# Residual and second-layer sums added by accumulating GpSimd DMAs, in a fused state-space and Mish feed-forward kernel

## The chip, the cores and the metric

The kernel runs on one core of one Trainium2 chip. The metric is the device time of one execution in microseconds; the time before is 371.92 us, the median of three runs (371.62 to 372.28). The engines are TensorE (PE in the profile, with PEld for its weight loads), VectorE (DVE), ScalarE (ACT), GpSimd (POOL) and SyncE (SP), which only issues DMAs.

## The reference

A sequence x of 2048 rows and 640 channels is normalized over the channels; two branches of the normalized rows are added to x: an S4D state-space convolution and a dense layer, Mish, dense layer.

```python
def _A_ref(u, log_A_real, A_imag, C_real, C_imag, log_dt, D_skip):
    ...
    P = jnp.exp((A * dt[:, None])[:, :, None] * pos[None, None, :])
    K = 2.0 * jnp.einsum("dn,dnl->dl", C, P).real
    ...
    return y + u * D_skip[None, None, :]      # y: causal convolution of u with K
...
def _B_ref(x, w1, b1, w2):
    h = jnp.einsum("bsd,df->bsf", x, w1) + b1
    sp = jnp.log1p(jnp.exp(-jnp.abs(h))) + jnp.where(h > 0, h, jnp.zeros_like(h))
    act = h * jnp.tanh(sp)
    return jnp.einsum("bsf,fd->bsd", act, w2)
...
x = A_u
xn = _layernorm(x, axis=-1)
return x + _A_ref(xn, ...) + _B_ref(xn, ...)
```

The layers are 640 to 1728 and 1728 to 640. With the given parameters the convolution's kernel is so smooth that a branch of the program replaces it by running sums: two prefix sums per channel with two coefficients. A flag computed from the parameters decides at the end whether a general branch has to run; here it does not.

## The kernel before

**Tiling.** All work is held transposed: channels or hidden units on the 128 partitions, rows of the sequence along the free dimension. The sequence is cut into four blocks b of 512 rows (TB), the 640 channels into five tiles k of 128 (KD), the 1728 hidden units into 14 chunks f (NF; one of them has 64). A step (b, f) is one hidden chunk of one block. Every float32 operand of a matmul is split into a high and a low float16 part, and three products (high-high, low-high, high-low) are summed, so that a step has 15 matmuls of 512 columns for the first layer (mm1) and 15 for the second (mm2).

**Order within a step.** The program order on each engine is written out by hand in step(b, f): the loads of that step (lists LOADS, all on SP), mm1(b, f), mm2 of the chunk three steps earlier (LAG = 3), the Mish operations of chunk f and the rest of those of chunk f - 1, and the lists V_, A_ and W_, in which place() puts side work for DVE and ACT. Engines are in-order queues. In the first three steps of a block mm2 still finishes the last three chunks of the block before; in step 2 the last of them, so that the five accumulators ACC[k] (one PSUM bank each) are then complete sums of the block before. The mm2 of the new block's first chunk overwrites them in step 3, after mm1(b, 3).

**Joining.** In step 2 of a block, join(b - 1, k) empties ACC[k]. For most tiles it adds ACC[k] / SO to RES[b, k], a buffer of 128x512 float32 into which SP loaded the residual x in good time (load_res). For the tiles in the set EARLY it is drain: it adds ACC[k] / SO to the tile XT[b][:, k], which by then holds everything else, and SP stores the result to the output.

**The skip work (state-space branch and residual).** XT[b][:, k] holds the normalized, transposed rows. For each of the 20 tiles, at the steps listed in CONV, four functions run:

- skip_a, a step before on ACT: two scaled copies g1 and g0 of XT, and the carry from the block before;
- skip_b on DVE: the first prefix sum, in g1, and XT = XT * D + RES, where RES holds x, or x and the second layer's sum if the join came first;
- skip_c on DVE: the second prefix sum, in g0, and XT = XT + g0; if the tile isn't EARLY, SP stores XT to the output;
- skip_d, a step later on ACT: the new carries.

CONV puts the tiles of block 0 at steps (1, 4) to (1, 7) and (2, 0), those of block 1 at (2, 3) to (2, 7), those of block 2 at (2, 13) and (3, 3) to (3, 6), those of block 3 at (3, 7) to (3, 11). EARLY are the tiles whose skip work lies in their own block: (2, 0) and all of block 3.

**The next block's rows.** In steps 2 to 5 of a block DVE takes mean and variance of the next block's rows (stats). In step 5 rstds() runs three small operations on GpSimd (lines 404, 405 and 743): 1/sigma by a power, and a copy of the means. In step 7, behind mm1, PE transposes that row of statistics (spread, line 411), ACT copies it out, and SP writes it to DRAM and reads it back broadcast to all partitions (bc). From step 8 on DVE normalizes one tile of XT a step with it (norm_t), and the float16 parts of the next block follow (hi_x, lo_x). In the middle of the program GpSimd does nothing else.

**The end.** Behind the last step PE finishes the last chunks tile by tile; drain empties each of the five tiles of block 3 when its accumulator is complete, the last one in two halves, and SP stores them.

Of the kernel before, what the change touches and what calls it, by code (L numbers as in the profile page):

```python
# [13 lines left out]
F32 = mybir.dt.float32  # L14
F16 = mybir.dt.float16
I32 = mybir.dt.int32
AF = mybir.ActivationFunctionType
OP = mybir.AluOpType
AX = mybir.AxisListType

P = 128
# [4 lines left out]
TB = 512  # L26
NB = L // TB
NT = TB // P
KD = D // P
# [3 lines left out]
LAST = NF - 1  # L33
HALF = 8
LAG = 3
# [12 lines left out]
SH, SO = SX * S1, SA * S2  # L48
# [238 lines left out]
def body(ctx: ExitStack, tc: tile.TileContext, x, xT, logA, Aim, Cr, Ci, logdt, vec, w1, w1T, w2, w2T, out):  # L287
    nc = tc.nc
    v, a, pe, sp, g = nc.vector, nc.scalar, nc.tensor, nc.sync, nc.gpsimd
# [11 lines left out]
    row = pool("row", 2)  # L301
# [19 lines left out]
    cc = cst.tile([P, 6, KD], F32, name="cc")  # L321
# [23 lines left out]
    ACC = [ps.tile([P, TB], F32, name=f"acc{k}") for k in range(KD)]  # L345
    W1S, W2S, XT, RES, XROW, ACT, SM, NX, CHK, SK, ML = ({} for _ in range(11))
    NCHK = NF + 3 * KD

    def load_w1(f, queues=(sp,)):
        W1S[f] = row.tile([P, KD, P], F32, name="w1s", tag="w", bufs=8)  # L350
        n, m = FC[f], P // len(queues)
        for j, e in enumerate(queues):
            o = D * FO[f] + j * m * KD * n
            e.dma_start(W1S[f][j * m:(j + 1) * m, :, :n], w1[o:o + m * KD * n].rearrange("(p k f) -> p k f", p=m, k=KD))

    def load_w2(f):
        W2S[f] = row.tile([P, D], F32, name="w2s", tag="w", bufs=8)
        n = FC[f]
        sp.dma_start(W2S[f][:n], w2[FO[f]:FO[f] + n])
        if n < P:  # L360
            sp.dma_start(W2S[f][n:2 * n], w2[FO[f]:FO[f] + n])

    def load_x(b, i):
        XROW[b, i] = row.tile([P, D], F32, name="xrow", tag="x", bufs=4)
        sp.dma_start(XROW[b, i], xr[b, i])

    def load_res(b, k):
        RES[b, k] = row.tile([P, TB], F32, name="res", tag="r", bufs=7)
        sp.dma_start(RES[b, k], xT[k * P:(k + 1) * P, b * TB:(b + 1) * TB])


    def hi_w1(f):
        n = FC[f]
        a.activation(W1H[f][:, :, :n], W1S[f][:, :, :n], AF.Copy, scale=S1)

    def lo_w1(f, e=v):
        n = FC[f]
        e.scalar_tensor_tensor(W1L[f], W1S.pop(f)[:, :, :n], S1, W1H[f][:, :, :n], op0=OP.mult, op1=OP.subtract)

    def hi_w2(f):  # L380
        a.activation(W2H[f], W2S[f], AF.Copy, scale=S2)

    def lo_w2(f, e=v):
        e.scalar_tensor_tensor(W2L[f], W2S.pop(f), S2, W2H[f], op0=OP.mult, op1=OP.subtract)

    def hi_x(b, k):
        a.activation(XH[b % 2][k], XT[b][:, k], AF.Copy, scale=SX)
# [5 lines left out]
    def xt_alloc(b):  # L393
        XT[b] = big.tile([P, KD, TB], F32, name="xt", tag="big" + "ACBA"[b])
# [30 lines left out]
    def load_par():  # L425
        t = big.tile([P, 4, KD, NS], F32, name="par", tag="bigB")
        for j, src in enumerate((logA, Aim, Cr, Ci)):
            sp.dma_start(t[:, j], src.rearrange("(k p) n -> p k n", p=P))
        return t
# [76 lines left out]

    def skip_b(b, k):
        g1, _ = SK[b, k]
        xt = XT[b][:, k]
        v.tensor_tensor_scan(g1[:, 1:], g1[:, 1:], zero.to_broadcast([P, TB]), car[:, 1, k:k + 1], op0=OP.add, op1=OP.add)  # L510
        v.scalar_tensor_tensor(xt, xt, cc[:, 3 * (b == 0) + 2, k:k + 1], RES.pop((b, k)), op0=OP.mult, op1=OP.add)  # L511

    def skip_c(b, k):
        g1, g0 = SK[b, k]
        v.tensor_tensor_scan(g0, g0, g1[:, 0:TB], car[:, 0, k:k + 1], op0=OP.add, op1=OP.add)  # L515
        v.tensor_tensor(XT[b][:, k], XT[b][:, k], g0, op=OP.add)
        if (b, k) not in EARLY:
            sp.dma_start(out[k * P:(k + 1) * P, b * TB:(b + 1) * TB], XT[b][:, k])

    def skip_d(b, k):  # L520
        g1, g0 = SK.pop((b, k))
        a.copy(car[:, 1, k:k + 1], g1[:, TB:])
        a.copy(car[:, 0, k:k + 1], g0[:, TB - 1:])
# [123 lines left out]
    def drain(b, k, src, t=slice(0, TB)):  # L647
        z = XT[b][:, k, t]
        v.scalar_tensor_tensor(z, src[:, t], 1 / SO, z, op0=OP.mult, op1=OP.add)
        sp.dma_start(out[k * P:(k + 1) * P, b * TB + t.start:b * TB + t.stop], z)  # L650

    def join(b, k):
        if (b, k) in EARLY:
            drain(b, k, ACC[k])
        else:
            v.scalar_tensor_tensor(RES[b, k], ACC[k], 1 / SO, RES[b, k], op0=OP.mult, op1=OP.add)

    E_, A_, V_, W_ = ({(b, f): [] for b in range(NB) for f in range(NF)} for _ in range(4))  # L660
    LOADS = {(b, f): [] for b in range(NB) for f in range(NF)}
    PEX = {}

    def place():
        for f in range(NF):

            if f + 6 < NF:
                LOADS[0, f].append(lambda f=f: load_w1(f + 6))
            if f + 2 < NF:
                LOADS[0, f].append(lambda f=f: load_w2(f + 2))  # L670
            A_[0, f].append(lambda f=f: hi_w2(f))
            if f + 4 < NF:
                A_[0, f].append(lambda f=f: hi_w1(f + 4))
            if f > 0 and f + 3 < NF:
                V_[0, f].append(lambda f=f: lo_w1(f + 3))
            V_[(0, f + 1) if f < LAST - 1 else (1, f - LAST + 1)].append(lambda f=f: lo_w2(f))

        LOADS[0, 4].append(lambda: SM.update(ops=mode_ops(load_par())))
        for at, n in (((0, 6), 13), ((0, 7), 15), ((1, 0), 8), ((1, 1), 99)):
            W_[at].append(lambda n=n: [o() for _, o in zip(range(n), SM["ops"])])  # L680

        LOADS[1, 0].append(lambda: xt_alloc(0))
        for k, f in enumerate((0, 0, 1, 1, 3)):
            V_[1, f].append(lambda k=k: v.tensor_tensor(XT[0][:, k], XH[0][k], XL[0][k], op=OP.add))

        for b in range(NB - 1):
            for i in range(NT):
                LOADS[b, i].append(lambda b=b, i=i: load_x(b + 1, i))
                W_[b, i + 2].append(lambda b=b, i=i: stats(b + 1, i))
            LOADS[b, 5].append(lambda b=b: load_xt(b + 1))  # L690
            W_[b, 5].append(rstds)
            PEX[b, 7] = spread
            for k in range(KD):
                W_[b, 8 + k].append(lambda b=b, k=k: norm_t(b + 1, k, NX["bc"]))
                (E_ if k == KD - 1 else A_)[b, 9 + k].insert(0, lambda b=b, k=k: hi_x(b + 1, k))
                (V_ if k == KD - 1 else W_)[b, 9 + k].insert(0, lambda b=b, k=k: lo_x(b + 1, k))

        n = [(b, f) for b in range(1, NB) for f in range(NF)][2:]
        for j in range(NCHK):
            LOADS[n[max(j - 3, 0)]].append(lambda j=j: load_chk(j))  # L700
            A_[n[j]].append(lambda j=j: chk(j))
        W_[n[NCHK]].append(lambda: [o() for o in chk_end()])
        PEX[n[NCHK + 2]] = ok_sum
        W_[n[NCHK + 2]].append(ok_end)

        for b in range(1, NB):
            for k in range(KD):
                (V_ if k < 3 else W_)[b, LAG - 1].append(lambda b=b, k=k: join(b - 1, k))

        for at, c, k in CONV:  # L710
            b, f = at
            prev = (b, f - 1) if f else (b - 1, LAST)
            nxt = (b, f + 1) if f < LAST else (b + 1, 0)
            if c == b:
                LOADS[b, f - 2].append(lambda c=c, k=k: load_res(c, k))
            A_[prev].append(lambda c=c, k=k: skip_a(c, k))
            V_[at].append(lambda c=c, k=k: skip_b(c, k))
            W_[at].append(lambda c=c, k=k: skip_c(c, k))
            A_[nxt].insert(0, lambda c=c, k=k: skip_d(c, k))
        for b in range(NB - 1):  # L720
            for k in range(KD):
                if (b, k) not in EARLY:
                    LOADS[b, LAST].append(lambda b=b, k=k: load_res(b, k))

    CONV = [((1, 4 + k), 0, k) for k in range(4)] + [((2, 0), 0, 4)] + [((2, 3 + k), 1, k) for k in range(KD)]
    CONV += [((2, 13), 2, 0)] + [((3, 2 + k), 2, k) for k in range(1, KD)] + [((3, 7 + k), 3, k) for k in range(KD)]
    EARLY = {(c, k) for (b, _), c, k in CONV if c == b}

    def stats(b, i):
        if i == 0:  # L730
            NX["mv"] = tmp.tile([P, NT, 2], F32, name="mv")
            NX["st"] = tmp.tile([P, 2, NT], F32, name="st_row")
        for o in stat_ops(NX["mv"], XROW.pop((b, i)), i):
            o()
# [183 lines left out]
    b, k = NB - 1, KD - 1  # L918
# [47 lines left out]
```

## Time and profile before

| what | value |
|---|---|
| time, median of three runs | 371.92 us (371.62 to 372.28) |
| the profiled execution's own time | 371.5 us |
| its span, first to last instruction | 369.6 us |
| granted TensorE clock, mean | 0.996 |
| DMA moved | 40.81 MB, mean 110 GB/s |
| DMA queue of SP (q1): share of the 16 engines' time | 33.8% |

A row of a group names the line, the engine, the operation, the tile written and the tiles read with partitions x elements, the count, the busy time in us, the mean ns of one, and the idle time of the engine just before them with what ended most of it. A row of waits names who waited for whom: us in total, times, the longest. A row of a stage gives its length, busy time and count of PE, PEld, DVE, ACT and POOL, the granted clock, the share of DMA and GB/s. A row of a timeline gives start and length in us; what stands in brackets is the idle time before it and what ended it. A matmul of 512 columns is shown as 0.38 us long, but the next starts some 0.22 us after it, since they are pipelined.

### The profile page before, as it was taken

How to read it: one execution, taken by the hardware profiler on the slowest of the kernel's cores; microseconds unless marked ns; L12 is line 12 of the kernel's file. 1: busy time of each engine (PE TensorE's matmuls, PEld its weight loads, DVE VectorE, ACT ScalarE, POOL GpSimd, SP SyncE). 2: the span in 40 equal slices, each digit the busy share in tenths (PEclk: the TensorE clock that was granted, in tenths of full speed). 3: DMA queues.
4: the chain of work that ended last, by engine and by line, in shares of the span. 5: the costliest groups of instructions: out<-in, count | busy, mean ns of one | idle time of the engine just before them, and what ended most of it. 6: DMA issues, size and time to landing. Idle time of an engine off the chain costs nothing.

```text
span 369.6 us, 4857 instructions
## 1 busy us (share of the span) xinstructions
PE 360.2 (97%) x1729; PEld 167.7 (45%) x1729; DVE 283.7 (77%) x484; ACT 267.7 (72%) x518; POOL 11.0 (3%) x22
## 2 busy tenths in 40 slices
PE   6999999999999999999999999999999999999993
PEld 5754444444444444444444444444444444444441
DVE  5969868995786998657558999766755899899723
ACT  3599896995757877876858878777767686798630
POOL 2100100000000030000000020000000000000000
PEclk9999999999999999999999999999999999999998
DMA  7967952850002165213552264413400021300004
GB/s 237 300 193 233 332 170 77 288 205 2 1 2 72 41 229 164 60 51 94 185 166 67 61 192 133 149 32 93 147 0 31 0 78 67 114 0 2 0 2 147
DMA packets 23102, 40.81 MB, mean 110 GB/s; under 512 B 3144, under 2 KB 6496, under 8 KB 23072
## 3 DMA queue, kind: packets, MB, share of 16 engines
q1 hardware_dynamic: 22464, 39.45, 33.8%
q10 hardware_dynamic: 608, 0.98, 0.8%
q8 instruction: 15, 0.25, 0.3%
q14 instruction: 15, 0.12, 0.1%
HBM read 35.17 MB, written 5.26 MB: 109 GB/s over the span
## 4 chain that ended last, share of the span: by engine, by line
PE 95%; DVE 2%; DMA 1%; ACT 1%; issue 0%; POOL 0%
PE h L556 45%; PE acc L583 14%; PE acc L585 14%; PE acc L584 14%; PE h L535 1%; PE acc L578 1%; PE acc L567 1%; PE acc L577 1%; PE acc L580 1%; DMA x<-in_A_u_dram 1%; PE tr L535 1%; PE acc L571 1%; PE acc L815 0%; ACT xh L818 0%; DVE st L398 0%
## 5 line engine op out<-in xcount | busy, mean ns | idle before, releaser
L556 PE MATMUL h<-xh,w1h 128*128 128x512 f16 x265 | 92.1, 380 | 0.0
L584 PE MATMUL acc<-lo,w2h 128*128 128x512 f16 x235 | 89.1, 379 | 0.0
L583 PE MATMUL acc<-hi,w2h 128*128 128x512 f16 x235 | 89.1, 379 | 0.0
L585 PE MATMUL acc<-hi,w2l 128*128 128x512 f16 x235 | 89.1, 379 | 0.0
L556 PE MATMUL h<-xh,w1l 128*128 128x512 f16 x245 | 86.4, 379 | 0.0
L608 ACT ACTIVATE s<-h,cv 128x512 f32<-128x512 f32 x51 | 34.9, 684 | 61.9 <-PE h L556 60.7
L556 PEld LDWEIGHTS <-w1h 128*128 128x128 f16 (+1 forms) x534 | 50.5, 98 | 63.7 <-issue 4.6
L612 DVE SCALAR_TENSOR_TENSOR A<-h,bs,s 128x512 f32<-128x512 f32 x51 | 38.0, 746 | 42.3 <-ACT s L608 42.1
L556 PE MATMUL h<-xl,w1h 128*128 128x512 f16 (+2 forms) x269 | 63.8, 377 | 0.0
L644 DVE SCALAR_TENSOR_TENSOR lo<-A,hi 128x512 f16<-128x512 f32 x52 | 35.7, 687 | 16.1 <-ACT hi L634 16.1
L620 ACT ACTIVATE p<-p,kc 128x512 f32<-128x512 f32 (+1 forms) x56 | 40.4, 722 | 1.7
L616 ACT ACTIVATE p<-s,kc 128x512 f32<-128x512 f32 (+1 forms) x56 | 39.8, 710 | 0.1
L624 ACT ACTIVATE s<-p,kc 128x512 f32<-128x512 f32 (+1 forms) x56 | 39.8, 710 | 0.0
L628 DVE SCALAR_TENSOR_TENSOR A<-s,A 128x512 f32<-128x512 f32 (+1 forms) x56 | 38.1, 681 | 1.6 <-ACT s L624 1.5
L556 PEld LDWEIGHTS <-w1l 128*128 128x128 f16 x245 | 24.0, 98 | 28.6
L634 ACT ACTIVATE hi<-A 128x512 f16<-128x512 f32 (+1 forms) x56 | 34.5, 615 | 2.4 <-DVE A L628 2.4
L583 PEld LDWEIGHTS <-w2h 128*128 128x128 f16 x235 | 23.1, 98 | 27.7
L585 PEld LDWEIGHTS <-w2l 128*128 128x128 f16 x235 | 23.0, 98 | 27.8
L584 PEld LDWEIGHTS <-w2h 128*128 128x128 f16 x235 | 23.0, 98 | 27.3
L510 DVE TENSOR_TENSOR_SCAN g<-g,car,kc 128x512 f32<-128x512 f32 x20 | 25.6, 1279 | 0.0
L515 DVE TENSOR_TENSOR_SCAN g<-g,car,g 128x512 f32<-128x512 f32 x20 | 25.3, 1264 | 0.0
L511 DVE SCALAR_TENSOR_TENSOR xt<-xt,cc,res 128x512 f32<-128x512 f32 x20 | 14.5, 725 | 0.0
(138 smaller groups left out, 339.6 us busy)
## 6 DMA issues: line engine op xcount, KB each, us to landing
res<-in_xT_dram SPq DMA_DIRECT2D x20, 256.0 KB, 5.1
out_dram<-xt SPq DMA_DIRECT2D x19, 256.0 KB, 2.7
chk<-in_w2T_dram SPq DMA_DIRECT2D x15, 288.0 KB, 3.4
w2s<-in_B_w_dram SPq DMA_DIRECT2D x13, 320.0 KB, 3.2
chk<-in_w1T_dram SPq DMA_DIRECT2D x13, 320.0 KB, 3.6
xrow<-in_A_u_dram SPq DMA_DIRECT2D x12, 320.0 KB, 4.3
xt<-in_xT_dram SPq DMA_DIRECT2D x15, 256.0 KB, 5.6
w1s<-in_w_dram SPq DMA_DIRECT2D x11, 320.0 KB, 4.9
```

Of the source, the lines that this page charges most:

```text
L556: pe.matmul(o, w, x, start=(j == 0), stop=(j == len(order) - 1))
L583: pe.matmul(ACC[k], W2H[f][:, c[k]], hi, start=False, stop=False)
L584: pe.matmul(ACC[k], W2H[f][:, c[k]], lo, start=False, stop=False)
L585: pe.matmul(ACC[k], W2L[f][:, c[k]], hi, start=False, stop=en)
L608: a.activation(s, h, AF.Sigmoid, bias=cv[:n, f:f + 1], scale=1 / SH)
L612: v.scalar_tensor_tensor(A, h, bs[:n, f:f + 1], s, op0=OP.add, op1=OP.mult)
L616: a.activation(p, s, AF.Arctan, bias=one[:n], scale=-1.0)
L620: a.activation(p, p, AF.Square, bias=pi4[:n], scale=2.0)
L624: a.activation(s, p, AF.Tanh, bias=mb[:n], scale=MG)
L628: v.scalar_tensor_tensor(A, s, MC, A, op0=OP.add, op1=OP.mult)
L634: a.activation(hi[:n], A, AF.Copy, scale=MA * SA / SH)
L644: v.scalar_tensor_tensor(lo, A, MA * SA / SH, hi[:n], op0=OP.mult, op1=OP.subtract)
```

## The change

The residual x and the second layer's sum no longer pass through DVE. A DMA issued by GpSimd with accumulation adds its source to the bytes at its destination.

- load_res goes. add_x(t, b, k) adds x from DRAM onto a tile t.
- join for a tile that isn't EARLY copies ACC[k] / SO into a new RES buffer, on DVE for k of 0 and 1, on ACT for k of 2, 3 and 4, and add_x adds x to it. All these joins are in step 2, those of DVE in V_, those of ACT in A_; before, three were in V_ and two in W_, all on DVE.
- skip_b keeps only its prefix sum. skip_c does XT = XT * D + g0 in one operation.
- finish(b, k) is new: GpSimd adds RES onto XT by an accumulating DMA, waits for it, and issues the store to the output, which was SP's. It stands behind skip_c of the tile, or, where the skip work comes before the join (tile (2, 0)), in step 2 of the next block.
- EARLY is block 3 alone; there skip_c is followed by add_x onto XT, and the drain at the end is as before.

On GpSimd's queue this makes, in order: the statistics of block 1; five add_x in step (1, 2); finish (0, 0) in (1, 4); the statistics of block 2, in (1, 5); finish (0, 1) to (0, 4); five add_x in (2, 2); finish (1, 0) and (1, 1), in (2, 3) and (2, 4); the statistics of block 3, in (2, 5); finish (1, 2) to (1, 4); five add_x in (3, 2); finish (2, 0) to (2, 4); five add_x onto XT of block 3.

PE's instructions and their order are the same as before.

```diff
-    def load_res(b, k):
-        RES[b, k] = row.tile([P, TB], F32, name="res", tag="r", bufs=7)
-        sp.dma_start(RES[b, k], xT[k * P:(k + 1) * P, b * TB:(b + 1) * TB])
+    def add_x(t, b, k):
+        g.dma_start(t, xT[k * P:(k + 1) * P, b * TB:(b + 1) * TB], accum_op=OP.add)
...
     def skip_b(b, k):
         g1, _ = SK[b, k]
-        xt = XT[b][:, k]
         v.tensor_tensor_scan(g1[:, 1:], g1[:, 1:], zero.to_broadcast([P, TB]), car[:, 1, k:k + 1], op0=OP.add, op1=OP.add)
-        v.scalar_tensor_tensor(xt, xt, cc[:, 3 * (b == 0) + 2, k:k + 1], RES.pop((b, k)), op0=OP.mult, op1=OP.add)
 
     def skip_c(b, k):
         g1, g0 = SK[b, k]
         v.tensor_tensor_scan(g0, g0, g1[:, 0:TB], car[:, 0, k:k + 1], op0=OP.add, op1=OP.add)
-        v.tensor_tensor(XT[b][:, k], XT[b][:, k], g0, op=OP.add)
-        if (b, k) not in EARLY:
-            sp.dma_start(out[k * P:(k + 1) * P, b * TB:(b + 1) * TB], XT[b][:, k])
+        z = XT[b][:, k]
+        v.scalar_tensor_tensor(z, z, cc[:, 3 * (b == 0) + 2, k:k + 1], g0, op0=OP.mult, op1=OP.add)
+        if (b, k) in EARLY:
+            add_x(z, b, k)
+
+    def finish(b, k):
+        z = XT[b][:, k]
+        g.dma_start(z, RES.pop((b, k)), accum_op=OP.add)
+        g.dma_start(out[k * P:(k + 1) * P, b * TB:(b + 1) * TB], z)
...
     def join(b, k):
         if (b, k) in EARLY:
             drain(b, k, ACC[k])
+            return
+        r = RES[b, k] = row.tile([P, TB], F32, name="res", tag="r", bufs=7)
+        if k < 2:
+            v.tensor_scalar(r, ACC[k], 1 / SO, None, op0=OP.mult)
         else:
-            v.scalar_tensor_tensor(RES[b, k], ACC[k], 1 / SO, RES[b, k], op0=OP.mult, op1=OP.add)
+            a.activation(r, ACC[k], AF.Copy, scale=1 / SO)
+        add_x(r, b, k)
...
-                (V_ if k < 3 else W_)[b, LAG - 1].append(lambda b=b, k=k: join(b - 1, k))
+                (V_ if k < 2 else A_)[b, LAG - 1].append(lambda b=b, k=k: join(b - 1, k))
...
-            if c == b:
-                LOADS[b, f - 2].append(lambda c=c, k=k: load_res(c, k))
             A_[prev].append(lambda c=c, k=k: skip_a(c, k))
             V_[at].append(lambda c=c, k=k: skip_b(c, k))
             W_[at].append(lambda c=c, k=k: skip_c(c, k))
+            if c < b:
+                W_[at].append(lambda c=c, k=k: finish(c, k))
+            elif (c, k) not in EARLY:
+                W_[b + 1, LAG - 1].append(lambda c=c, k=k: finish(c, k))
             A_[nxt].insert(0, lambda c=c, k=k: skip_d(c, k))
-        for b in range(NB - 1):
-            for k in range(KD):
-                if (b, k) not in EARLY:
-                    LOADS[b, LAST].append(lambda b=b, k=k: load_res(b, k))
...
-    EARLY = {(c, k) for (b, _), c, k in CONV if c == b}
+    EARLY = {(c, k) for (b, _), c, k in CONV if c == NB - 1}
```

## The prediction

> **What bounds the kernel now.** I read the page first (busy time, slices, chain), then who waited for whom, then stages, and last the timelines of the places that the change touches. The page:
>
> ```profile
> span 369.6 us, 4857 instructions
> PE 360.2 (97%) x1729; PEld 167.7 (45%) x1729; DVE 283.7 (77%) x484; ACT 267.7 (72%) x518; POOL 11.0 (3%) x22
> PE 95%; DVE 2%; DMA 1%; ACT 1%; issue 0%; POOL 0%
> ```
>
> PE is busy 97% of the span and makes 95% of the chain that ended last. Pipelined matmuls can look busy while they wait, so the waits of PE come next; these rows are all that it has:
>
> ```profile
> PE acc L815 <- DVE x L799: 1.7, 3, 1.0
> PE tr L829 <- POOL car L328: 1.4, 1, 1.4
> PE h L535 <- ACT w1h L374: 0.2, 1, 0.2
> ```
>
> Lines 815, 829 and 535 belong to the start-up. After it PE waits for nobody, and its clock is whole (0.72 only where it has nothing left to do). By stage (busy time, counts, PEclk, DMA share, GB/s):
>
> ```profile
> 0.00:12.50 12.50, 9.08 (x57) 7.19 (x57) 8.10 (x28) 5.06 (x10) 3.40 (x13) 1.00 0.81 247
> 206.00:226.00 20.00, 20.00 (x94) 9.08 (x93) 19.79 (x29) 15.96 (x36) 2.93 (x3) 1.00 0.50 149
> 319.00:339.00 20.00, 20.00 (x94) 9.03 (x93) 19.01 (x25) 15.84 (x33) 0.00 (x0) 1.00 0.01 4
> 341.00:357.00 16.00, 16.00 (x76) 7.24 (x75) 9.94 (x14) 9.48 (x18) 0.00 (x0) 1.00 0.00 1
> 364.00:369.60 5.60, 0.00 (x0) 0.00 (x0) 0.32 (x1) 0.00 (x0) 0.00 (x0) 0.72 0.41 140
> ```
>
> Three stages speak for the whole middle. Where DVE works 19.8 of 20 us beside 149 GB/s of DMA, and where it works 19.0 of 20 beside 4 GB/s, PE does the same 94 matmuls in 20 us; where DVE is at 62% (9.94 of 16) it does 76 in 16, 95 in 20. So PE's rate does not depend on DVE or on the DMA traffic. The time is about 12.5 us of start, 351 us of saturated PE, and the 6 us after its last matmul:
>
> ```profile
> 363.31 0.27 PE L596 MATMUL h<-lo,w2h 128*128 128x256 f16 x1
> 363.58 0.74 DVE L649 SCALAR_TENSOR_TENSOR xt<-h,xt 128x256 f32<-128x256 f32 x2
> 360.45 5.62 SPq L650 DMA_DIRECT2D out_dram<-xt  x6
> ```
>
> **The change, part by part.**
>
> *DVE work taken away.* The groups:
>
> ```profile
> L511 DVE SCALAR_TENSOR_TENSOR xt<-xt,cc,res 128x512 f32<-128x512 f32 x20 | 14.5, 725 | 0.0
> L516 DVE TENSOR_TENSOR xt<-xt,g 128x512 f32<-128x512 f32 x20 | 13.8, 692 | 0.7
> L656 DVE SCALAR_TENSOR_TENSOR res<-acc,res 128x512 f32<-128x512 f32 x14 | 8.8, 679 | 0.0
> ```
>
> The 20 skip_b operations of 725 ns go, and the 20 additions of 692 ns become the scaled-addition form of 725 ns: 14.5 - 0.7 = 13.8 us less. Of 15 joins (these 14 and one drain of the same kind) nine leave DVE: 9 x 0.68 = 6.1 us. DVE loses about 20 of 284 us. Worth on the end: nothing, since no wait of PE after the start ends with DVE. Bounds: zero, and a gain only from stalls that the profile does not show (second rival).
>
> *Three joins a block on ScalarE.* No row has an ACT copy of 128x512 float32 out of PSUM. Nearest: the copy of 64x512 from PSUM, 582 ns, and the scaled copy of 128x512 from SBUF, 713 ns. I take 0.65 us, three in a row 2.0 us (1.7 to 2.1). The place, in block 1:
>
> ```profile
> 109.57 0.19 ACT L473 ACTIVATION_READ_ACCUMULATOR sq<-chk 128x1 f32 x1
> 112.33 0.69 ACT L608 ACTIVATE s<-h,cv 128x512 f32<-128x512 f32 x1 [2.57 <-PE h L556]
> 112.99 0.38 PE L577 MATMUL acc<-hi,w2h 128*128 128x512 f16 x1
> 200.40 0.69 ACT L608 ACTIVATE s<-h,cv 128x512 f32<-128x512 f32 x1 [1.31 <-PE h L556]
> L604 ACT COPY A<-h 64x512 f32<-64x512 f32 x4 | 2.3, 582 | 2.1 <-PE h L556 2.1
> L503 ACT ACTIVATE g<-xt,cc 128x512 f32<-128x512 f32 x20 | 14.3, 713 | 0.0
> ```
>
> ACT stands idle 2.57 us there, and the copies fit. The first ends near 110.4, and PE overwrites that bank (accumulator 2) at 112.99; the copies of 3 and 4 follow 0.65 us later each, PE's overwriting two matmuls later each (2 x 20/94 = 0.43 us), so the least slack is 2.1 us. In blocks 2 and 3 the two skip copies stand behind the joins and the idle time is 1.31 us; queued behind them are the next sigmoid and, through it, DVE's A. They come about 0.5 us late for one step, and the next steps' idle ACT time takes it up; PE uses that activation only three steps later. Cost nothing; if the cover were gone, at most 0.7 us at each of two places.
>
> *Loads and stores leave SP.* 20 residual loads and 15 output stores go from SP to POOL. Nothing on SP is then held by a store's wait for DVE; its remaining issues come earlier, into buffers that are free. Worth nothing to PE.
>
> *50 DMAs on POOL's queue.* Here the change adds a wait. For each of 15 tiles POOL now issues an accumulation, waits until it has landed, and issues the store. Behind that on the same in-order queue stand the three small operations that make the next block's 1/sigma, and PE itself waits for these with a transpose:
>
> ```profile
> 125.54 0.69 DVE L516 TENSOR_TENSOR xt<-xt,g 128x512 f32<-128x512 f32 x1
> 131.14 1.00 POOL L404 TENSOR_SCALAR st_row<-mv 128x4 f32<-128x4 f32 x1 [86.84 <-DVE mv L400]
> 133.70 0.45 POOL L743 COPY st_row<-mv 128x4 f32<-128x4 f32 x1
> 138.03 0.27 PE L411 MATMUL tr<-ident,st_row 128*8 128x128 f32 x1
> 207.13 0.69 DVE L516 TENSOR_TENSOR xt<-xt,g 128x512 f32<-128x512 f32 x1
> 213.74 0.69 DVE L516 TENSOR_TENSOR xt<-xt,g 128x512 f32<-128x512 f32 x1
> 219.34 1.01 POOL L404 TENSOR_SCALAR st_row<-mv 128x4 f32<-128x4 f32 x1 [85.19 <-DVE mv L400]
> 221.91 0.45 POOL L743 COPY st_row<-mv 128x4 f32<-128x4 f32 x1
> 226.10 0.27 PE L411 MATMUL tr<-ident,st_row 128*8 128x128 f32 x1
> ```
>
> Today the row of statistics is ready at 134.15 and 222.36, 3.9 and 3.7 us before PE takes it. Call c the time from an accumulation's issue to the end of the store's issue behind it. In block 1 one such pair (step 4) stands ahead of the three operations. It starts when skip_c ends, at 125.54 + 0.69 - 0.6 (the operation gone from that step) = 125.6; then c, then the three operations, 3.0 us (131.14 to 134.15): in time if c is at most 138.0 - 125.6 - 3.0 = 9.4 us. In block 2 two pairs stand there (steps 3 and 4). The first starts near 207.7 (one operation less, but ACT's 0.5 us), the second at 213.7 or when the first is through: in time if 207.7 + 2c + 3.0 is at most 226.1, c at most 7.7 us. The third boundary, block 0 to 1, has no such DMA ahead of it, and block 3 has no next block.
>
> c has no row. Nearest are the DMAs of 256 KB, KB and us to landing, among them those that add_x replaces:
>
> ```profile
> out_dram<-xt SPq DMA_DIRECT2D x19, 256.0 KB, 2.7
> bc<-sd SPq DMA_DIRECT2D x6, 256.0 KB, 3.3
> xt<-in_xT_dram SPq DMA_DIRECT2D x15, 256.0 KB, 5.6
> 207.85 0.34 SPq L518 DMA_DIRECT2D out_dram<-xt  x1
> 42.80 0.23 POOL L404 TENSOR_SCALAR st_row<-mv 128x4 f32<-128x4 f32 x1 [29.95 <-DVE mv L400]
> ```
>
> Lower end: the store, 2.7, and an issue of 0.34: c = 3.0. Upper end: an accumulation reads its destination too, so twice the slowest, 11.2, and an issue as long as POOL's slowest instruction, the one between the rows of 131.14 and 133.70, 1.5 us: c = 12.7. The slow 5.6 comes from five loads issued together; the pairs of a step stand alone, so I go by the lighter rows, about 4 us to landing, and 1 us for each of two issues: c = 6. That is under both limits, by 3.4 and 1.7 us. Cost: 0, with the slack in block 2 nearly used. At the upper end: 12.7 - 9.4 = 3.3 us in block 1 and 2 x 12.7 - 15.4 = 10.0 us in block 2.
>
> POOL's own instruction of 128x4 took 0.23 us at 42.80 and 1.00 us at 131.14, beside a DVE that was then scanning without a break: POOL is stretched by DVE, and so may its DMA issues be. [...]
>
> *The end.* The last additions of x (block 3, steps 7 to 11) start by 345.4 at the latest (344.75 + 0.69, below), and the drain that needs them first is the one at 359.73: 14 us, above the upper c. The 6 us behind PE keep their operations.
>
> ```profile
> 344.75 0.69 DVE L516 TENSOR_TENSOR xt<-xt,g 128x512 f32<-128x512 f32 x1
> 359.73 0.69 DVE L649 SCALAR_TENSOR_TENSOR xt<-acc,xt 128x512 f32<-128x512 f32 x1 [4.01 <-PE acc L596]
> ```
>
> **Sum.** DVE 0, ACT 0, SP 0, POOL 0, end 0: the profiled execution's 371.5 us (span 369.6 and 1.9 around it) stays. It lies 0.4 us under the median of the runs shown, 371.92; I predict on the median, 371.9 us. A change under 0.2% (0.74 us) is what a measurement of this kernel can't tell from none.
>
> **Rivals.**
>
> *POOL comes late (slower).* Place: the transpose of the statistics in step 7 of blocks 1 and 2; it decides from c = 7.7 in block 2, 9.4 in block 1. For it: the thin 1.7 us, the stretched POOL rows, an unknown accumulation. Against: lone transfers of 256 KB land in 2.7 to 3.3 us. At c = 9 the second transpose waits 2 x 9 - 15.4 = 2.6 us: 374.5 us. At c = 10.5 it is 1.1 + 5.6: 378.6.
>
> *Hidden stalls go (faster).* DVE runs for 19.8 of 20 us in one stage, and runs without a profile may have short stalls from it that this one lacks. The most that this can hold is the slowest run shown over the profiled one, 372.28 - 371.5 = 0.8 us: 371.1. Against it: no PE wait in the middle at all.
>
> *The joins on ACT or the last additions are late (slower).* ACT twice 0.7 us: 373.3; it needs the 2.1 us of slack at the banks gone, for which nothing speaks.
>
> **How the numbers follow.** Forecast, no change: 0.57. POOL late: 0.32. Hidden stalls: 0.09. ACT or end: 0.02. Faster 0.09, same 0.57, slower 0.34. The range goes from 371.1, the faster rival, to 375.6 (c = 9.5), which leaves out the upper third of the POOL case. The forecast's own range is 371.2 to 372.6.
>
> **What would show it.** Right: no PE wait after the start, transposes still at about 138.0 and 226.1, POOL's statistics ending before them, DVE near 264 us busy, ACT near 274. Wrong: a wait of PE or of the transpose's weight load for POOL at line 404 or 749 (the new number of 743), a wait of PE for ACT at line 577, pairs on POOL longer than 7.7 us, or a rate under 94 matmuls in 20 us.

## The result: 1 us more, and where the profile after shows it

| | before | after |
|---|---|---|
| median, runs beside each other (14 each) | 371.67 us (371.18 to 372.28) | 372.72 us (372.21 to 373.75) |
| ratio, 95% interval | | 1.003 (1.0021 to 1.0039) |
| profiled execution: time / span / time outside the span | 371.50 / 369.59 / 1.91 | 372.37 / 370.20 / 2.17 |
| last matmul ends | 363.58 | 363.53 |
| last DMA lands | 368.07 | 368.12 |
| from the last landing to the end of the span | 1.52 | 2.09 |

The change costs about 1 us, which is small and yet outside what the measurement leaves to chance. The last three rows show where it is: in the two profiled executions PE ends and the last store lands within 0.05 us of before, and only what follows is longer. The page after, in the lines that answer to those of before:

```profile
span 370.2 us, 4877 instructions
PE 361.0 (98%) x1729; PEld 168.5 (46%) x1729; DVE 268.4 (72%) x455; ACT 271.5 (73%) x527; POOL 50.9 (14%) x72
PE 95%; DMA 2%; issue 0%; ACTq 0%; ACT 0%; DVE 0%
```

DVE has lost 15.3 us of work, POOL has gained 39.9 (most of it issues), and PE still makes 95% of the chain. Its waits after:

```profile
PE tr L835 <- POOL car L328: 1.5, 1, 1.5
PE acc L821 <- DVE x L805: 0.5, 2, 0.3
PE tr L538 <- ACT w1h L373: 0.3, 1, 0.3
PE h L538 <- ACT w1h L373: 0.2, 1, 0.2
```

These rows belong to the start-up; behind it PE waits for nobody, as before. The stages that the prediction looked at (busy time and counts of PE, PEld, DVE, ACT, POOL, then PEclk, DMA share, GB/s):

```profile
0.00:12.50 12.50, 10.02 (x57) 7.95 (x58) 8.16 (x28) 5.06 (x10) 3.46 (x13) 1.00 0.80 246
206.00:226.00 20.00, 20.00 (x94) 9.04 (x93) 18.53 (x26) 15.97 (x36) 7.24 (x8) 1.00 0.72 193
319.00:339.00 20.00, 20.00 (x95) 9.03 (x93) 17.34 (x21) 15.64 (x34) 2.79 (x4) 1.00 0.29 53
341.00:357.00 16.00, 16.00 (x76) 7.26 (x75) 9.37 (x13) 9.38 (x18) 0.88 (x1) 1.00 0.19 30
364.00:370.20 6.20, 0.00 (x0) 0.00 (x0) 0.27 (x1) 0.00 (x0) 0.00 (x0) 0.85 0.37 124
```

Where DVE works 1.3 to 1.7 us less of 20 and the DMA moves 193 instead of 149 GB/s, or 53 instead of 4, PE does the same 94 or 95 matmuls. Only the last row is longer: 6.20 us without a matmul against 5.60 before. The timeline of the end and the last 2.2 us by window, and below them the last window of before:

```profile
363.26 0.27 PE L599 MATMUL h<-lo,w2h 128*128 128x256 f16 x1
363.52 0.75 DVE L652 SCALAR_TENSOR_TENSOR xt<-h,xt 128x256 f32<-128x256 f32 x2
364.06 1.95 SPq L653 DMA_DIRECT2D out_dram<-xt  x2
...
368.00:369.00 1.00, 0.00 (x0) 0.00 (x0) 0.00 (x0) 0.00 (x0) 0.00 (x0) 0.69 0.00 0
369.00:370.20 1.20, 0.00 (x0) 0.00 (x0) 0.00 (x0) 0.00 (x0) 0.00 (x0) 0.50 0.00 0
...
369.00:369.60 0.60, 0.00 (x0) 0.00 (x0) 0.00 (x0) 0.00 (x0) 0.00 (x0) 0.50 0.00 0
```

The last window is 0.6 us shorter in before. In these windows no engine is busy and the DMA moves 0 GB/s, so the page has no name for this time. The trace's semaphore records have it (a semaphore shows there as a numbered counter that engines and landing DMAs raise and that instructions wait for). When the last stores have been issued, SP in both traces waits in turn for the eight semaphores that its own DMAs raise (100 to 108 without 101), then goes down a second list, two semaphores an entry; then SP, ACT, DVE and PE wait on one semaphore (97) that POOL raises, the barrier of the table, and POOL clears a range of semaphores. In us from the start of the span; the first row gives landings with their semaphores, the others SP's entries and the closing:

```
                         before                                  after
last three landings      367.17(104) 367.76(105) 368.07(106)     367.02(100) 367.90(102) 368.12(103)
SP waits, first list     100 102 103 | 104 367.19, 105 367.78,   100 367.04, 102 367.92, 103 368.13,
                         106 368.09, 107 368.15, 108 368.22      104 368.22, 105 368.29, 106 368.36,
                                                                 107 368.43, 108 368.50
second list              8 entries, 368.29 to 368.73             12 entries, 368.56 to 369.24
barrier, range clear     369.01, 369.16 (135 ns)                 369.53, 369.72 (178 ns)
last entry               369.53                                  370.14
```

Two things have changed there. The last store used the sixth of SP's eight DMA semaphores before and uses the third after. Both traces walk the list in the order 100 to 108, so five entries instead of two are still to be walked when that store lands, at about 0.07 us each. And the second list has four entries more: the program now has GpSimd DMAs, and in the trace of after these raise eight semaphores of their own (111 to 118). Whether these two are the cause, and whether the joins, the DMA traffic or DVE's freed time take part, is what the runs had to tell. From here on, the closing is the time from the last landing to the end of the span.

### The profile page after: what moved, and what is told of

Same layout as the page of the kernel before. It is cut to its first block, busy times and chain, and to the rows that moved or that the text cites. A ratio compares the mean times of both kernels' runs of the same rounds, so it can differ in the third digit from the quotient of the medians.

```text
span 370.2 us, 4877 instructions
## 1 busy us (share of the span) xinstructions
PE 361.0 (98%) x1729; PEld 168.5 (46%) x1729; DVE 268.4 (72%) x455; ACT 271.5 (73%) x527; POOL 50.9 (14%) x72
## 4 chain that ended last, share of the span: by engine, by line
PE 95%; DMA 2%; issue 0%; ACTq 0%; ACT 0%; DVE 0%
PE h L559 45%; PE acc L586 14%; PE acc L587 14%; PE acc L588 14%; DMA w1s<-in_w_dram 2%; PE h L538 1%; PE acc L581 1%; PE acc L570 1%; PE acc L583 1%; PE acc L580 1%; PE tr L538 1%; PE acc L574 1%; PE acc L821 0%; PE acc L599 0%; PE acc L596 0%
## 5 line engine op out<-in xcount | busy, mean ns | idle before, releaser
L368 POOL DMA_DIRECT2D res<-in_xT_dram x15 | 13.5, 992 | 123.8 <-DVE res L661 113.1
```

## The experiments

Theory A: the time is lost in the closing of the program, by the number of semaphores and by the place of the last store among them. Theory B: it is lost to the traffic of the accumulating DMAs. Theory C: it comes from the joins on ScalarE and the new order on DVE. All times are medians; the ratio is to the runs of the kernel before on the same chip, with its 95% interval; "landing to end" is read from the profiled execution as in the table above.

| kernel | median (runs) | ratio | landing to end | outside the span, median |
|---|---|---|---|---|
| before_sw1 | 371.80 (11) | 1.0000 (0.9991 to 1.0008) | 1.64 | 1.80 |
| before_sw8 | 372.17 (11) | 1.0009 (1.0001 to 1.0018) | 1.83 | 1.83 |
| after_nodma | 372.01 (12) | 1.0001 (0.9991 to 1.0011) | 1.53 | 1.78 |
| after_hw5 | 372.13 (11) | 1.0005 (0.9996 to 1.0014) | 1.72 | 1.90 |
| after_again | 372.75 (8) | 1.0027 (1.0017 to 1.0038) | 2.09 | 2.17 |
| after_hw8 | 372.58 (11) | 1.0024 (1.0015 to 1.0033) | 2.09 | 2.08 |
| before_hw2 | 371.63 (11) | 0.9998 (0.9988 to 1.0007) | 1.44 | 1.80 |
| after_late | 379.01 (3) | 1.0197 (1.0180 to 1.0215) | 2.09 | 2.41 |
| before_sw8_hw5 | 372.37 (11) | 1.0017 (1.0008 to 1.0026) | 2.05 | 1.80 |
| after_pool3 | 372.46 (6) | 1.0024 (1.0012 to 1.0036) | 2.09 | 2.17 |
| after_act3 | 373.57 (2) | 1.0054 (1.0035 to 1.0073) | 2.09 | 2.22 |
| after_hw16 | 372.55 (8) | 1.0027 (1.0016 to 1.0038) | 2.09 | 2.04 |

The kernel before has a median of 371.87 (35 runs) beside the first four, 371.62 (24) beside the next four and 371.70 (24) beside the last four; outside its span lie 1.85 to 1.87 us.

### One and eight small GpSimd DMAs in the kernel before

```diff
+        for j in range(1):        # before_sw8: range(8)
+            W_[2, 9].append(lambda j=j: g.dma_start(padt[:, j:j + 1], vec[:, j:j + 1]))
```

They load 128x1 numbers in the middle of block 2 into a tile that nobody reads.

> The kernel before with one extra DMA on GpSimd's queue (128 x 4 bytes into a tile that nobody reads, step (2, 9)). Theory A (the change costs its time behind the last matmul: the program's end waits for and clears the semaphores of GpSimd's DMAs, and GpSimd as a DMA issuer makes the wrap-up behind the span longer): PE ends at 363.5 us as before; one more wait of about 0.06 us in SP's closing list; the time outside the span shows whether the 0.3 us come with the first such DMA. Time +0.1 to +0.4 us over the kernel before. Theory B (the traffic of 50 DMAs of 256 KB slows something): no difference, within 0.1 us. Theory C (the ScalarE joins or DVE's new order): no difference.

> The kernel before with eight such tiny DMAs on GpSimd's queue, one for each of the eight semaphores that its DMAs rotate over. Theory A: PE ends at 363.5 us; SP's closing list of waits has 12 entries in place of 8 (+0.25 us), the clearing of semaphores takes 0.18 in place of 0.135 us, the span grows by 0.35 us, the time outside the span by 0.3: +0.65 us in all, 372.3 us. Theory B and theory C: no difference, within 0.1 us.

Eight such loads move 4 KB and still lengthen the closing from 1.52 to 1.83 us. In the trace of before_sw8 the second list has the 12 entries of after and the range clear takes 178 ns. That is 0.31 us for eight small GpSimd DMAs and their semaphores. One such load costs 0.12 in the closing, where 0.06 was expected: one entry more in the list, and a range clear that takes 178 ns with one load already. Its median can't be told from before. The 0.3 us outside the span that theory A expected as well came with neither kernel (1.80 and 1.83). But 0.31 is only half of 0.57, so the count of semaphores alone doesn't explain the kernel after.

### The kernel after without its GpSimd DMAs

```diff
-        if (b, k) in EARLY:
-            add_x(z, b, k)
...
-        g.dma_start(z, RES.pop((b, k)), accum_op=OP.add)
-        g.dma_start(out[k * P:(k + 1) * P, b * TB:(b + 1) * TB], z)
+        RES.pop((b, k))
+        sp.dma_start(out[k * P:(k + 1) * P, b * TB:(b + 1) * TB], z)
...
-        add_x(r, b, k)
...
+        for j in range(4):
+            LOADS[2, 9].append(lambda j=j: sp.dma_start(padt[:, j:j + 1], vec[:, j:j + 1]))
```

The joins on DVE and ACT and DVE's shorter skip work stay; the four small loads put the last store back on the sixth semaphore.

> The changed kernel without any GpSimd DMA: the second layer's sums of blocks 0 to 2 and the residual x are left out of the output, the 15 stores go from SP, and four tiny loads on SP keep the rotation of SP's semaphores as in the kernel before. The ScalarE joins and the shorter DVE work stay. Theory A: the kernel before to within 0.1 us, 371.7 us, end of the span behind the last matmul 6.0 us. Theory B: the same, 371.7. Theory C (joins or DVE order cost): stays near 372.7 us. If the 20 us less on DVE were worth anything, it would be below 371.5.

The page of after_nodma, and its window of block 2:

```profile
span 369.8 us, 4810 instructions
PE 360.9 (98%) x1729; PEld 168.5 (46%) x1729; DVE 268.4 (73%) x455; ACT 271.5 (73%) x527; POOL 10.6 (3%) x22
...
206.00:226.00 20.00, 20.00 (x95) 9.09 (x93) 18.64 (x26) 15.96 (x36) 2.73 (x3) 1.00 0.51 149
```

DVE and ACT are exactly as busy as in after (268.4 and 271.5), the time is that of before, and the closing takes 1.53 us. So theory C falls: the joins, the new order and 15 us less on DVE together change the time by less than 0.4 us, the half-width of the interval. A cost of the joins and an equal gain from DVE would look the same in this run; the profile, without a wait of PE behind the start, speaks for neither. The run does not yet decide between A and B, since it takes out the traffic and the semaphores together; before_sw8, which has the semaphores without the traffic, shows A's first half.

### The rotation: where the last store falls among eight semaphores

SP's DMAs take its eight semaphores in turn: in the traces of before and after their issues name 107, 108, 100, 102, 103, 104 and so on to the last store. The change takes 35 DMAs from SP (20 residual loads and 15 stores), and 35 = 4 x 8 + 3, so every later one moves three places back: sixth to third. Small loads on SP in block 2 turn it further, by 5 to the eighth place, by 8 or 16 to where it was; in the kernel before, 2 give the eighth.

```diff
+        for j in range(5):        # after_hw8: 8, after_hw16: 16; before_hw2: 2
+            LOADS[2, 9].append(lambda j=j: sp.dma_start(padt[:, j:j + 1], vec[:, j:j + 1]))
```

> The changed kernel with five tiny loads more on SP (128 x 4 bytes, step (2, 9)), so that the last store uses the last of SP's eight semaphores in place of the third. Theory A: SP's first closing list waits for the semaphores in their order at 0.07 us each; behind the last landing none is left in place of five, so the span shrinks by about 0.35 us, time 372.4 us. Theory B: no difference from the changed kernel, 372.7 us. Theory C: no difference, 372.7 us.

> The changed kernel once more, beside the three below and the kernel before on one chip. Theory A (end of the program: eight more semaphores, 0.3 us; the last store's place in SP's list, 0.25 us; something behind the span, 0.3 us): ratio 1.002 to 1.004, last landing to end of span 2.08 us, time outside the span 2.2 us. If the 0.3 us outside the span belonged to the chip or the day, 1.8 us outside the span and a ratio near 1.0015.

> The changed kernel with eight tiny loads more on SP: SP's program is longer, but the last store uses the same semaphore as in the changed kernel (eight is a whole turn). Theory A: last landing to end of span 2.08 us, as in the changed kernel and not 1.72 as with five. If the 0.3 us outside the span hang on the length of SP's program, they go here (1.8 to 1.9 outside) and the ratio is near 1.0015; if they belong to the change itself, 2.2 outside and a ratio of 1.003. Theory B (traffic): as the changed kernel, 1.003.

> The kernel before with two tiny loads more on SP, so that the last store uses the last of the eight semaphores. Theory A: none of SP's first list is left behind the last landing in place of two: last landing to end of span 1.38 us in place of 1.52, time 0.14 us under the kernel before (ratio 0.9996, too little to tell by the times alone). Theory B and C: 1.52 us, no difference.

> The changed kernel with 16 tiny loads more on SP (two whole turns of its semaphores). If the 0.3 us behind the span hang on where SP's program ends, they move again: with 5 more the distance from span to time was 1.90, with 8 more 2.08, with none 2.17. Last landing to end of span 2.08 by theory A.

With five more loads on SP the kernel after, all its 50 GpSimd DMAs in place, has a closing of 1.72 instead of 2.09 us and a ratio of 1.0005 whose interval holds 1. This is where theory B falls too: the whole traffic is there, and the time is not (the interval leaves room for at most 0.5 us). The last matmul says the same: it ends at 363.29 to 364.01 us in the profiled executions of the six kernels with all of the change's DMAs and PE unhindered (after, after_again, after_hw5, after_hw8, after_hw16, after_pool3), and at 363.21 to 364.15 in those of before and its four variants. This spread is also why the closing, which repeats to 0.01 us, tells more than a single time. With 8 or 16, a full turn, the closing is 2.09 to the hundredth and the ratio is again 1.0024 or 1.0027; for the closing the number of loads is not what counts, their remainder by eight is. The unchanged kernel after, run again beside these, repeats the first result. In the kernel before, the eighth place shortens the closing from 1.52 to 1.44, where 1.38 was expected: SP's last entry does come 0.13 us sooner behind the landing (1.33 against 1.46), but the span ends 0.11 us behind that entry instead of 0.06. The time doesn't follow it visibly (0.9998, interval from 0.9988 to 1.0007): 0.08 us is below what these runs can tell.

Both halves put into the kernel before:

```diff
+        for j in range(5):
+            LOADS[2, 9].append(lambda j=j: sp.dma_start(pad2[:, j:j + 1], vec[:, j:j + 1]))
+        for j in range(8):
+            W_[2, 9].append(lambda j=j: g.dma_start(padt[:, j:j + 1], vec[:, j:j + 1]))
```

> The kernel before with eight tiny GpSimd DMAs and five tiny loads on SP: all the work of before, but the changed kernel's set of semaphores and its last store on the third of SP's eight. Theory A: last landing to end of span 2.06 us as in the changed kernel (1.52 before; 1.83 with the GpSimd DMAs alone), time 0.55 us over the kernel before, ratio 1.0015, and 1.0025 if the 0.3 us behind the span come too. Theory B (the traffic of the accumulations): the kernel before with the eight, 1.0009 or less.

Five loads take the last store from the sixth place to the third, as in after. Nothing of the change is in this kernel; it has the closing of after (2.05 against 2.09) and loses 0.17% (0.08 to 0.26). Its parts add up: 1.44 with nothing behind the landing, 5 x 0.07 for five entries behind it, and 0.28 to 0.31 for GpSimd's semaphores (1.72 - 1.44, 1.83 - 1.52) give 2.07 to 2.10.

### What lies outside the span

The ratio of before_sw8_hw5 is 1.0017, that of after 1.0030 and 1.0027. About 0.3 us of after are still missing, and the table has them: outside the span lie 2.17 to 2.19 us in after and 1.80 to 1.90 in before and its variants. This part is behind the span, too: the trace has semaphore records there. Semaphore 2 is raised 18 times, from 0.52 to 2.02 us behind the end of the span in before and from 0.33 to 2.29 in after; in between nearly every semaphore from 7 to 255 has one record, in blocks that start apart, three of them of 51 (54 to 104, 105 to 155, 156 to 206). The last records of semaphore 2, in us behind the end of the span:

```
before           ... 1.66 1.70 1.74 1.78 1.80 | 1.90 1.94 1.97 2.02
before_sw8_hw5   ... 1.64 1.67 1.71 1.76 1.78 | 1.88 1.92 1.95 2.00
after_hw5        ... 1.63 1.67 1.71 1.77 1.80 | 1.89 1.93 1.97 2.01
after            ... 1.55 1.58 1.62 1.67 1.69 | 2.17 2.21 2.24 2.29
after_again      ... 1.55 1.58 1.62 1.67 1.69 | 2.17 2.21 2.24 2.29
```

One step (at the bar) takes 0.48 us in after instead of 0.10. Two more variants of after asked whether the length of POOL's or of ACT's program decides it.

```diff
+        for j in range(3):        # after_pool3; after_act3: A_[2, 9], a.copy(padt[:, j:j + 1], cv[:, j:j + 1])
+            W_[2, 9].append(lambda j=j: g.memset(padt[:, j:j + 1], 0.0))
```

> The changed kernel with three memsets of 128x1 more on GpSimd in step (2, 9). For the 0.3 us behind the span alone (2.17 us from span to time in the changed kernel, 1.8 to 1.9 in others): if they hang on where GpSimd's program ends, 1.8 to 1.9 here; if on the change's work or on another engine's program, 2.17. Last landing to end of span 2.08 by theory A either way.

> The changed kernel with three copies of 128x1 more on ScalarE in step (2, 9). If the 0.3 us behind the span hang on where ScalarE's program ends, 1.8 to 1.9 us from span to time here; else 2.17. Last landing to end of span 2.08 by theory A.

Neither moves it: 2.17 and 2.22 us, with the same step of 0.48 in both traces. Five more loads on SP do move it, to 1.90 and a step of 0.10. Eight and sixteen remove that step as well (0.10 in both traces), but the median outside stays at 2.08 and 2.04. In both their traces the records of another block of 51 end 0.5 us later; yet the profiled execution with sixteen has only 1.91 us outside, so this doesn't explain the medians. after_late, described below, adds accumulations on GpSimd and nothing on SP. It has no step of 0.48 either (0.10, but two others of 0.16 and 0.14 where after has 0.04), and still 2.41 us outside. So this part changes with the program, with SP's and with GpSimd's; GpSimd DMAs as such don't bring it (1.83 and 1.80 in before_sw8 and before_sw8_hw5). What makes the step long, and what else lengthens this part, stays open.

(after_act3 has only two runs, and in its profiled execution PE ends 1.2 us later than in after, with longer waits in the start-up, one of them `PE h L538 <- ACT xh L827: 0.8, 1, 0.8`. It is used for the end alone.)

### The deadline on POOL, with each accumulation done twice

The forecast's main rival was that POOL's pairs of accumulation and store hold up the statistics of the next block. In the kernel after they don't. To see whether the place and the price were right, each accumulation of finish is done twice:

```diff
-        g.dma_start(z, RES.pop((b, k)), accum_op=OP.add)
+        r = RES.pop((b, k))
+        g.dma_start(z, r, accum_op=OP.add)
+        g.dma_start(z, r, accum_op=OP.add)
```

> The changed kernel with each accumulation of the second layer's sum onto the tile done twice, one behind the other (the output holds that sum twice for blocks 0 to 2). It tests the deadline that the prediction worked out: a pair on GpSimd's queue took 4.1 us in block 1 and 8.75 and 4.8 us in block 2, and the statistics ended 5.0 and 1.2 us before the transpose. With one accumulation more (some 3.5 us) per pair they end near 136.6 (still in time) and 224.8 + 7 = 231.8: PE waits for GpSimd some 5 to 6 us at the transpose of block 2 and nowhere else; time 377 to 379 us. If the transpose has more slack than that reading, no wait and 373 us.

PE's wait in the profile of after_late, and POOL's and PE's timelines there:

```profile
PE tr L410 <- POOL st_row L751: 4.5, 1, 4.5
...
208.55 0.87 POOL L521 DMA_DIRECT2D xt<-res  x1 [1.94 <-DVE A L617]
220.73 0.58 POOL L523 DMA_DIRECT2D out_dram<-xt  x1 [3.36 <-DMA xt<-res]
228.56 0.58 POOL L523 DMA_DIRECT2D out_dram<-xt  x1 [2.79 <-DMA xt<-res]
230.50 0.18 POOL L751 COPY st_row<-mv 128x4 f32<-128x4 f32 x1
230.74 0.27 PE L410 MATMUL tr<-ident,st_row 128*8 128x128 f32 x1 [4.49 <-POOL st_row L751]
```

The deadline is where the prediction put it, at the transpose of block 2, and nowhere else: in block 1, with one pair, PE doesn't wait. The first pair of block 2 is through 12.8 us after its issue (208.55 to 221.31), the second after 7.8. Together they pass the 15.4 us that two pairs have by 5.2. The first starts 0.85 us later than the 207.7 of the estimate, and the three operations take 1.5 us instead of 3.0, with DVE idle beside them (0.7 us busy of the 6 from 225 to 231): 5.2 + 0.85 - 1.5 is the 4.5 us that PE waits. The run is 6.3 us slower than after (379.01 against 372.72), though, and the rest is in the stages behind the stall:

```profile
231.00:234.00 3.00, 3.00 (x10) 1.16 (x8) 2.09 (x3) 2.92 (x6) 0.57 (x1) 0.54 0.50 89
234.00:236.00 2.00, 2.00 (x9) 0.64 (x6) 2.00 (x3) 1.23 (x5) 0.86 (x1) 0.83 0.67 235
236.00:240.00 4.00, 4.00 (x23) 1.75 (x23) 1.83 (x4) 1.44 (x3) 0.00 (x0) 1.00 0.71 157
```

The granted clock is 0.54 for 3 us and 0.83 for 2, where the kernel after has 1.00, so 3 x 0.46 + 2 x 0.17 = 1.7 us of full-speed work are lost after the wait. In the window of 3 us PE does 10 matmuls; the kernel after does 15 in it.

## Why the prediction was wrong, step by step

**The step that failed is the end.** "The 6 us behind PE keep their operations", and the term was 0. The operations that the profile names do keep their times: last matmul, last drain and last landing are within 0.05 us. What the term left out is the program's closing, which the busy rows don't show. It measured 0.57 us in the profiled execution: about 0.3 from GpSimd's eight DMA semaphores (before_sw8), about 0.25 from the last store's move from the sixth to the third place (after_hw5, before_hw2, before_sw8_hw5). Outside the span, which the prediction carried over as "1.9 around it", came another 0.26. With the 0.05 of the landing these make 0.88, against 0.87 us between the two profiled executions. The medians lie 1.05 us apart; the other 0.2 is less than their interval can tell. The cause of the 0.57 is shown, that of the part outside the span stays open. The rows that were there for it: the span ends 1.5 us after the last landing, in windows with no engine busy and next to no DMA traffic, which is time with an owner although none is named. That 35 DMAs leave SP's queue and 50 come to POOL's was counted, but only for what they wait for. The forecast also took 0.2% as the least that can be told from no change; 14 runs of each kernel tell 0.3% with an interval of 0.09% to either side.

**DVE: 0. Right.** By the groups it lost what was worked out: 14.5 + 13.8 + 8.8 of before and one drain of 0.7 against 15.0 and 3.8 after, 19.0 us less where about 20 had been taken (the new form takes 752 ns, not 725).

```profile
L514 DVE SCALAR_TENSOR_TENSOR xt<-xt,cc,g 128x512 f32<-128x512 f32 x20 | 15.0, 752 | 0.7
L661 DVE TENSOR_SCALAR res<-acc 128x512 f32<-128x512 f32 x6 | 3.8, 683 | 0.0
```

The page's busy time fell by 15.3 only, to 268.4 and not 264: there, time in which two instructions overlap counts once (in before an addition of 0.69 us starts at 125.54 and the next operation at 126.15), so that a sum of durations can't be taken off it. after_nodma, with the same 268.4 and a ratio of 1.0001, shows no gain at the end.

**Joins on ACT: 0. Right.** A copy takes 582 ns, less than the 650 taken, and ACT was 271.5 us busy against 274 expected. In block 1 three copies are through at 111.15, before the next sigmoid may start:

```profile
109.61 1.54 ACT L663 ACTIVATE res<-acc 128x512 f32<-128x512 f32 x3
112.27 0.69 ACT L611 ACTIVATE s<-h,cv 128x512 f32<-128x512 f32 x1 [1.12 <-PE h L559]
200.37 0.69 ACT L611 ACTIVATE s<-h,cv 128x512 f32<-128x512 f32 x1
L663 ACT ACTIVATE res<-acc 128x512 f32<-128x512 f32 x9 | 4.6, 582 | 0.0
```

The 0.5 us of delay that was expected in block 2 did not come either: the sigmoid there starts at 200.37, against 200.40 before. Three copies of 1.54 us took just the idle time that there was.

**SP: 0. Right for PE, wrong for POOL.** The five loads of block 3's XT, freed from the stores ahead of them, start at 204.88 instead of 214.90. The prediction saw such loads come earlier "into buffers that are free" and gave that no price. PE pays none, but POOL's first pair in block 2 starts 2.8 us behind them. The first row is of before, the others are of after, with the pair of block 1 ahead of those of block 2:

```profile
214.90 2.30 SPq L739 DMA_DIRECT2D xt<-in_xT_dram  x5
...
126.26 0.88 POOL L520 DMA_DIRECT2D xt<-res  x1 [8.99 <-DMA chk<-in_w1T_dram]
129.78 0.58 POOL L521 DMA_DIRECT2D out_dram<-xt  x1 [2.64 <-DMA xt<-res]
204.88 3.14 SPq L745 DMA_DIRECT2D xt<-in_xT_dram  x5
207.65 0.86 POOL L520 DMA_DIRECT2D xt<-res  x1 [2.28 <-DVE xt L514]
215.82 0.58 POOL L521 DMA_DIRECT2D out_dram<-xt  x1 [7.30 <-DMA xt<-res]
216.45 0.85 POOL L520 DMA_DIRECT2D xt<-res  x1
220.70 0.58 POOL L521 DMA_DIRECT2D out_dram<-xt  x1 [3.39 <-DMA xt<-res]
221.29 0.62 POOL L403 TENSOR_SCALAR st_row<-mv 128x4 f32<-128x4 f32 x1
223.84 1.01 POOL L749 COPY st_row<-mv 128x4 f32<-128x4 f32 x1
226.04 0.27 PE L410 MATMUL tr<-ident,st_row 128*8 128x128 f32 x1
```

**POOL: 0. Right, with one size off and some luck.** The estimate was c = 6 us for a pair, with two issues added to the time to landing; but that time counts from the start of the issue, so that only the store's issue comes on top. It is 4.1 in block 1 (126.26 to 130.36), and in block 2 it is 8.75 (207.65 to 216.40) and 4.8 (216.45 to 221.28). The first of these is above the 7.7 us that the prediction allowed a pair, one of its own signs of being wrong; the two together, 13.6, are below 15.4. Had the second taken the estimated 6 us, the 1.2 us that were left at the end would have been gone. That the slow one is slow from the loads in flight is read from the timeline and wasn't tested by itself. The statistics are ready at 224.85, which is these 1.2 us before PE takes them, where 3.7 us were left before. after_late shows what that margin guards: the mechanism of the first rival was right, with its place, and the change stays just short of it. Its price was too low: the prediction counted the wait alone, and a wait of 4.5 us cost 6.3. Issues of accumulations took this:

```profile
L520 POOL DMA_DIRECT2D xt<-res x15 | 13.1, 871 | 56.5 <-DVE xt L514 47.0 <-DMA chk<-in_w1T_dram 9.0 <-issue 0.4
L521 POOL DMA_DIRECT2D out_dram<-xt x15 | 8.7, 580 | 52.3 <-DMA xt<-res 52.3
res<-in_xT_dram POOLq DMA_DIRECT2D x15, 256.0 KB, 5.7
xt<-res POOLq DMA_DIRECT2D x15, 256.0 KB, 3.3
xt<-in_xT_dram POOLq DMA_DIRECT2D x5, 256.0 KB, 4.3
```

An accumulation is issued in 0.87 us and lands in 3.3 (median), within the 1 and 4 that were taken. Beside a DVE that is busy 18.5 of 20 us (206 to 226 us) the two issues of block 2 took 0.86 and 0.85, so they were not stretched as the prediction thought they might be.

**The rivals.** POOL late: not here. Hidden stalls gone: after_nodma has the freed DVE and the joins on ACT without the DMAs and stands at 1.0001, so nothing of them shows. ACT or the last additions late: no. A rival for the closing was missing, and no term that was written down is behind the 0.3%.

## What to carry to other kernels

Moving DMAs between queues changed this program's tail, from 1.52 to 2.09 us, with the last landing in place to within 0.05: count which DMA semaphores a program uses and on which of them its last store falls, and read the time from the last landing to the end of the span, in the windows where nothing is busy. The first eight DMAs of an engine that had none cost here about 0.3 us, and each place of the last store short of the end of the list about 0.07; this matters only when less than 1% is at stake. An engine with 15 us less work, behind a PE that waits for nobody, gained nothing that these runs can tell, and the deadline of a small job behind a queue's waits is judged by the sum of those waits under the traffic that the same change sets free.

## What the runs showed that was not expected

- At the end of before and after SP walked its DMA semaphores in the same order, 100 to 108, and then a second list, at 0.06 to 0.09 us an entry; with 12 instead of 8 entries in the second list, and the last store on the third instead of the sixth of eight semaphores, the closing is 2.09 us instead of 1.52.
- Behind the span one step of semaphore 2 takes 0.48 us in some of these programs and 0.10 in others; it went from 0.48 to 0.10 with loads added on SP and with accumulations added on GpSimd, and not with three instructions added on POOL or ACT. The time outside the span doesn't follow this step alone.
- One wait of PE of 4.5 us cost 6.3 (after_late): the granted clock was 0.54 for 3 us behind it and 0.83 for 2 more. From 231.28 to 234.69 us matmuls start 0.43 us apart, and behind that 0.22 again. What length of wait is needed for this, no run shows.
- An accumulating DMA of 256 KB from SBUF to SBUF landed in 3.3 us (median of 15), from DRAM onto SBUF in 5.7 (15) and 4.3 (5); one that started while 5 loads of 256 KB were in flight took over 8 us.
- GpSimd's three small operations took 1.5 us beside an idle DVE (after_late, block 2) and 3.6 beside one busy for 18.5 of 20 us (after, block 2); the issues of its stores took 0.58 us in both.
